# A second level of the seven-product scheme inside the first layer of a fused attention and snake MLP kernel

## The chip, the cores and the metric

The kernel runs on one core of one Trainium2 chip. The metric is the device time of one execution in microseconds: 910.94 us before the change, the median of three runs from 910.55 to 911.62 us. One profiled execution of the same kernel has a span of 908.3 us from its first to its last instruction. All data are float32.

## The reference, cut to what matters

Attention over pooled keys and values comes first (8 batches, 8 heads, 576 queries of width 64, 72 pooled keys), then a two-layer network with a snake activation on 4608 tokens.

```python
def _attn_ref(q, k, v):                       # q, k, v: (8, 8, 576, 64)
    k_p = k.reshape(B, H, Sp, 8, D).mean(axis=3)
    v_p = v.reshape(B, H, Sp, 8, D).mean(axis=3)
    scores = scale * np.matmul(q, k_p.transpose(0, 1, 3, 2))
    attn = softmax(scores)                    # written out in the source
    return np.matmul(attn, v_p)

def _moe_ref(x, w_in, w_out, alpha):          # x: (4608, 512), d_ff = 2048
    h = x @ w_in
    s = np.sin(alpha * h)
    g = h + s * s / (alpha + 1e-09)
    return g @ w_out
```

## The kernel before

The kernel works in nine units of 512 tokens. While unit u runs the first layer (`hidden`), the attention of batch u + 1 is interleaved with it. Both layers use the seven-product (Strassen-Winograd) scheme: eight block products become seven, paid for by additions. In the first layer the weights are cut into 2 x 2 blocks of 256 x 1024 and the tokens of a unit into 2 x 256. A unit has four groups J of 256 hidden rows, and a group has seven products, so a unit has 28 products in 28 slots (slot = 7 J + k). One product is four matmuls of a 128 x 128 weight block with 256 columns.

The sums that the scheme needs are formed in PSUM: ScalarE (ACT) copies the bank of product 1 to a second bank, TensorE (PE) accumulates product 6 onto the copy, ACT copies that to a third bank for product 7, and so on.

```python
for slot in range(7 * self.NJ):
    J, k = divmod(slot, 7)
    for f in self.left: f()              # what the slot before left to do
    for f in extra[slot]: f()            # the attention of the next batch
    ...
    def left0(): G.b6 = bank(); nc.scalar.copy(out=G.b6[:], in_=G.b1[:]); squares(Q)
    def left1(): self.finish(Q)                              # VectorE additions
    def left2(): self.store_g(Q); G.b7 = bank()
                 nc.scalar.copy(out=G.b7[:], in_=G.b6[:])    # b7 copy
                 nc.scalar.copy(out=G.p5[:], in_=G.b5[:])    # p5 copy
    def left3(): sin(G, 0, 0, G.b1); square(G, 0, 0)
    def left4(): add(G.g[:, 1, :, 1], G.b7[:], G.p5[:])
    def left5(): add(G.g[:, 0, :, 1], G.b6[:], G.p5[:]); sin(G, 1, 1, ...); add(G.g[:, 0, :, 0], ...)
    def left6(): sin(G, 0, 1, G.g[:, 0, :, 1]); ...; sin(G, 1, 0, G.b7)
    p = (1, 5, 6, 2, 7, 3, 4)[k]
    product(p, bank of p, k < 2)          # 4 matmuls, 128 x 128 by 256 columns
```

(The blocks `left0` to `left6` are shortened; Q is the group before G.) So the b7 copy of a group stands on ACT at the start of slot k = 3, and product 7 on PE in slot k = 4.

The attention enters through a table of slots. In units 1 to 6:

```python
at((3, 5)[i], A.two_scores, i)            # i = 0, 1
at((8, 9, 10, 10)[i], A.exp, i)           # i = 0 .. 3
at((9, 10, 11, 12)[i], A.norm, i)
at((12, 12, 13, 13)[i], A.turn, i)
at(14, A.move, range(4))                  # SBUF to SBUF transfers aM <- tr
at(25, A.all_values)                      # slot 25 is J = 3, k = 4
at(26, self.att[b + 1].k_t)
at(7, self.load_q, u + 3)
for part in range(4): at(22 + part, self.turn_q, u + 2, part)
```

`all_values` multiplies the attention weights with the pooled values (PE) and then puts the result, scaled, into the tokens of the next units (`to_x`, nine ACT instructions in units 1 to 6):

```python
def all_values():
    ...
    halves(ps[2], main[2][0], True); rest_of((0, 1))
    (nc.vector.tensor_copy if b > 1 else nc.scalar.copy)(out=<order>, in_=rest[:, 1, 0:1])
    for hp in (0, 3, 1): halves(ps[hp], main[hp][0], True)
    rest_of((2, 3))
    for hp in hps:                         # the four last matmuls, 32 x 512
        nc.tensor.matmul(ps[hp], w, x, start=False, stop=True)
    for hp in hps: to_x(ps[hp], hp, 0, 512)
    to_x(rest, slice(0, 4), 512, 64)

def to_x(...):
    nc.scalar.mul(out=x, in_=y, mul=1.0 / POOL)
```

Of the kernel before, what the change touches and what calls it, by code (L numbers as in the profile page):

```python
# [19 lines left out]
P = 128  # L20
# [20 lines left out]
class Kernel:  # L41
# [33 lines left out]
    def new_q(self, b):  # L75
        self.qm[b] = self.qp.tile([P, 5 * self.H * self.D], F32, name="q")
# [6 lines left out]
    def pairs_q(self, b, tiles):  # L83

        nc = self.nc
        if 0 in tiles:
            self.raw = self.q_views(self.qm[b])
            self.qm[b] = self.qp.tile([P, 5 * self.H * self.D], F32, name="q")
        x = self.qm[b][:].rearrange("p (t h e d) -> p t e h d", t=5, e=2, d=self.D)
        for t in tiles:  # L90
            n = P if t < 4 else 64
            raw = self.raw[0][:, :, t, :] if t < 4 else self.raw[1]
            nc.scalar.copy(out=x[:n, t], in_=raw.rearrange("p (e h) d -> p e h d", e=2))
# [108 lines left out]
    def turn_q(self, b, part):  # L202


        nc = self.nc
        qm = self.qm[b]
        main, rest = self.q_views(qm)
        if part == 0:
            self.tr = self.new_tr()
        tr = self.tr[:, 0:2560].rearrange("p (k x) -> p k x", k=2)  # L210
        if part == 0:
            for e in range(2):
                x = main[:, 4 * e:4 * e + 4].rearrange("p hp t (k i) -> p hp t k i", i=32).rearrange("p hp t k i -> p (hp t) k i")
                out = tr[:, :, 768 * e:768 * e + 512].rearrange("p k (n i) -> p n k i", i=32)
                nc.vector.transpose(out=out, in_=x)
            return
        if part == 1:
            nc.vector.transpose(out=tr[:64, :, 512:768].rearrange("p k (n i) -> p n k i", i=32),
                                in_=self.q_rows(qm).rearrange("p (n k i) -> p n k i", k=2, i=32))
            return  # L220
        self.qt[b] = qm[:]
        for a in ((0, 1), (2, 3))[part - 2]:
            for c in range(4):
                e, k = divmod(c, 2)
                w = 768 if a == e else 512
                to = 512 if a == e == 1 else self.q_at(a)
                at = 512 if a == e == 1 else 768 * e
                nc.sync.dma_start(out=qm[32 * c:32 * c + 32, to:to + w], in_=tr[32 * a:32 * a + 32, k, at:at + w])
# [14 lines left out]
    def attention(self, b):  # L243
# [22 lines left out]
        def q_t(i, copy=nc.scalar.copy):  # L266
# [3 lines left out]
            if b not in self.qt:  # L270
                self.qt[b] = self.qt_view(self.qp.tile([P, 5 * H * D], F32, name="q"))
# [105 lines left out]
        def q_head(hp):  # L377

            if hp == 0:
                self.qt[b] = self.qt_view(self.qp.tile([P, 5 * H * D], F32, name="q"))  # L380
# [73 lines left out]
        def a_head(g, banks):  # L454

            aM, aR = a0_views()
            for e in range(2):
# [4 lines left out]
                cp(out=aM[:, 2 * g + e, 0:4 * P], in_=ps.rearrange("k t n -> k (t n)"))  # L462
            ps = self.psum([P, 4, P], banks[2])
# [32 lines left out]
        def move(blocks, queue=nc.sync):  # L496

            tr = self.tr[:, 0:2944].rearrange("p (c s x) -> p c s x", c=2, s=2)
            for a in blocks:
                for s in range(2):  # L500
                    for c in range(2):
                        r, w = 64 * s + 32 * c, 704 if c else 736
                        queue.dma_start(out=self.aM[r:r + 32, a, 0:w], in_=tr[32 * a:32 * a + 32, c, s, 0:w])  # L503
# [78 lines left out]
        def all_values():  # L582
# [16 lines left out]
            (nc.vector.tensor_copy if b > 1 else nc.scalar.copy)(out=self.sm.tile([P, 1], F32, name="order")[:], in_=rest[:, 1, 0:1])  # L599
# [158 lines left out]

    def sums_of_x(self, u, n):
# [9 lines left out]
    def hidden(self, u, extra):  # L769

        nc = self.nc
        bank = lambda: self.bank([P, JW, TH])
        add = lambda o, x, y: nc.vector.tensor_tensor(out=o, in0=x, in1=y, op=OP.add)  # L773

        for slot in range(7 * self.NJ):
            J, k = divmod(slot, 7)
            for f in self.left:
                f()
            for f in extra[slot]:
                f()  # L780
            if k == 0:
                before = self.group
                G = self.group = SimpleNamespace(
                    u=u, J=J, b1=bank(), g=self.hp.tile([P, 2, JW, 2, TH], F32, name="h"),
                    s=self.hp.tile([P, 2, JW, 2, TH], F32, name="s", bufs=1))
            xT, bt = self.xT[u], self.bt[u]
            B = lambda i, j: xT[:, 2 * i:2 * i + 2, j * TH:(j + 1) * TH]

            def product(p, ps, start):
                x = {1: B(0, 0), 2: B(1, 0), 3: B(1, 1), 4: bt[:, 3], 5: bt[:, 0], 6: bt[:, 1], 7: bt[:, 2]}[p]  # L790
                for jj in range(JW):
                    f = J * JW + jj
                    for kk in range(2):
                        nc.tensor.matmul(ps[:, jj, :], self.A[p][:, kk, f * P:(f + 1) * P], x[:, kk, :],  # L794
                                         start=(start and jj == 0 and kk == 0), stop=(kk == 1), skip_group_check=True)

            def sin(G, i, j, src):
                for jj in range(JW):
                    f = i * self.K2 // 2 + G.J * JW + jj
                    nc.scalar.activation(out=G.s[:, i, jj, j, :], in_=src[:, jj], func=AF.Sin, scale=self.al[:, f:f + 1])  # L800

            def square(G, i, js):

                for jj in range(JW):
                    f = i * self.K2 // 2 + G.J * JW + jj
                    x = G.s[:, i, jj, js, :]
                    nc.scalar.activation(out=x, in_=x, func=AF.Square, scale=self.c[:, f:f + 1])  # L807

            early = lambda G: G.J == (0 if G.u else 1)

            def squares(G):
                if not early(G):
                    square(G, 0, 1)
                square(G, 1, slice(0, 2))

            self.squares = squares

            def left0(G=G, Q=before):
                G.b6 = bank()
                nc.scalar.copy(out=G.b6[:], in_=G.b1[:])  # L820
                if Q:
                    squares(Q)

            def left1(G=G, Q=before):
                if Q:
                    self.finish(Q)

            late = G.J == 0 and 0 < u < self.B - 1

            def left2(G=G, Q=before, late=late):  # L830
                if Q and not late:
                    self.store_g(Q)
                G.b7 = bank()
                nc.scalar.copy(out=G.b7[:], in_=G.b6[:])
                G.p5 = self.tp.tile([P, JW, TH], F32, name="p5")
                nc.scalar.copy(out=G.p5[:], in_=G.b5[:])

            def left3(G=G):
                sin(G, 0, 0, G.b1)
                square(G, 0, 0)  # L840

            def left4(G=G):
                add(G.g[:, 1, :, 1], G.b7[:], G.p5[:])

            def left5(G=G, Q=before, late=late):
                if late:
# [3 lines left out]
                add(G.g[:, 0, :, 0], G.b1[:], G.s[:, 0, :, 0])  # L850

            def left6(G=G):
                sin(G, 0, 1, G.g[:, 0, :, 1])
                if early(G):
                    square(G, 0, 1)
                sin(G, 1, 0, G.b7)

            self.left = [(left0, left1, left2, left3, left4, left5, left6)[k]]
            if k == 1:
                G.b5 = bank()  # L860
            p = (1, 5, 6, 2, 7, 3, 4)[k]
            product(p, getattr(G, {1: "b1", 5: "b5", 6: "b6", 2: "b1", 7: "b7", 3: "b6", 4: "b7"}[p]), k < 2)

    def finish(self, Q):
        add = lambda o, x, y: self.nc.vector.tensor_tensor(out=o, in0=x, in1=y, op=OP.add)  # L865
        add(Q.g[:, 1, :, 0], Q.b7[:], Q.s[:, 1, :, 0])
        add(Q.g[:, :, :, 1], Q.g[:, :, :, 1], Q.s[:, :, :, 1])
# [7 lines left out]
    def end_hidden(self):  # L875
        nc, Q = self.nc, self.group
        for f in self.left:
            f()
        self.squares(Q)
# [3 lines left out]
    def first_batch(self):  # L883
# [70 lines left out]
        A.a_head(0, (1, 7, 0))  # L954
        self.combine_w_in(0, (0,), nc.gpsimd)
        A.products_head(3)
        A.soft_exp(2)
# [15 lines left out]
    def carry(self, u):  # L973
# [6 lines left out]
        if u == 0:  # L980
# [36 lines left out]
            at(20, A.move, (3,), nc.scalar)  # L1017
            at(26, A.all_values)
            at(9, self.load_q, 2)
            at(14, self.load_q, 3)  # L1020
# [8 lines left out]
        if 0 < u < last:  # L1029
# [18 lines left out]
            if u + 3 <= last:  # L1048
                at(7, self.load_q, u + 3)
# [3 lines left out]
        if turn and u + 2 <= last:  # L1053
            for part in range(4):
                at(turn + part, self.turn_q, u + 2, part)
# [23 lines left out]
    def outputs(self):  # L1079
# [55 lines left out]
        def early(st):  # L1135
# [4 lines left out]
            if st["u"] == self.B - 1:  # L1140
                out(st["u"], 0, 1, t, 5, queues=(nc.sync, nc.scalar))
# [4 lines left out]
        def out(u, i, j, t, n0=0, n1=2 * T // 32, queues=(nc.sync, nc.sync)):  # L1146
# [7 lines left out]
            for a in range(4):  # L1154
                c = j * 2 * P + a * 64
                queues[a % 2].dma_start(out=self.out[r + 32 * n0:r + 32 * n1, c:c + 64].rearrange("(n k) c -> k n c", k=32),
                                        in_=o[32 * a:32 * a + 32, n0:n1].rearrange("k n h c -> k n (h c)"))

        def combine(st):
# [35 lines left out]
            else:  # L1195
# [4 lines left out]
                else:  # L1200
                    out(u, 0, 1, t, 0, 5, (nc.sync, nc.scalar))
# [69 lines left out]
    def run(self):  # L1271
        nc, tc = self.nc, self.tc
        pool = lambda s, n, b, **kw: s.enter_context(tc.tile_pool(name=n, bufs=b, **kw))
        with ExitStack() as top:
# [10 lines left out]
            with ExitStack() as one:  # L1285
# [8 lines left out]
                self.qp = pool(att, "qp", 2)  # L1294
# [12 lines left out]
                self.last = cb.tile([64, 640], F32, name="last")  # L1307
# [7 lines left out]
                self.bt, self.left, self.group, self.turn = {}, [], None, 2  # L1315
                self.R = {}
                self.first_batch()
                for u in range(self.NU):
# [63 lines left out]
```

## Time and profile before

| what | value |
|---|---|
| time, median of 3 | 910.94 us |
| span of the profiled execution | 908.3 us |
| ACT busy | 436.4 us (48%) |
| VectorE (DVE) busy | 665.6 us (73%) |
| GpSimd (POOL) busy | 170.8 us (19%) |
| data moved by DMA | 141.12 MB, mean 155 GB/s |

The first layer runs from about 20 us to 527 us of the span, the second layer follows. In the profile L794 is the matmul of the first layer's products, L1129 that of the second layer, L302 the scores, L592 and L605 the values, L519 the rescaling by `to_x`, L820 the copy of b1 to b6, L834 the copy of b6 to b7, L836 the p5 copy, L773 and L865 the additions of the first layer on DVE, L800 and L807 the sines and squares, L503 the issue of the transfers aM <- tr. A float32 matmul shows as two records, so a product is eight records. Matmuls overlap: the pace is the distance of one start from the next, not the duration of one record.

### The profile page before, as it was taken

How to read it: one execution, taken by the hardware profiler on the slowest of the kernel's cores; microseconds unless marked ns; L12 is line 12 of the kernel's file. 1: busy time of each engine (PE TensorE's matmuls, PEld its weight loads, DVE VectorE, ACT ScalarE, POOL GpSimd, SP SyncE). 2: the span in 40 equal slices, each digit the busy share in tenths (PEclk: the TensorE clock that was granted, in tenths of full speed). 3: DMA queues.
4: the chain of work that ended last, by engine and by line, in shares of the span. 5: the costliest groups of instructions: out<-in, count | busy, mean ns of one | idle time of the engine just before them, and what ended most of it. 6: DMA issues, size and time to landing. Idle time of an engine off the chain costs nothing.

```text
span 908.3 us, 17532 instructions
## 1 busy us (share of the span) xinstructions
PE 898.3 (99%) x6906; PEld 814.3 (90%) x6906; DVE 665.6 (73%) x1000; ACT 436.4 (48%) x998; POOL 170.8 (19%) x159
## 2 busy tenths in 40 slices
PE   8999999999999999999999999999999999999997
PEld 5787888888888888888888999999999999999997
DVE  7675766748567584663557899979798888889895
ACT  5695775867668676686876621111111111111111
POOL 4785350703408044130000000000000000000000
PEclk9999999999999999999999999999999999999999
DMA  9985766758667575548117247161618162534401
GB/s 263 242 249 153 210 170 193 194 174 233 175 176 189 165 204 170 146 116 313 73 74 249 94 127 220 37 213 40 222 27 226 37 190 72 171 92 128 134 15 40
DMA packets 128746, 141.12 MB, mean 155 GB/s; under 512 B 46920, under 2 KB 95704, under 8 KB 128664
## 3 DMA queue, kind: packets, MB, share of 16 engines
q1 hardware_dynamic: 126488, 138.03, 52.9%
q10 hardware_dynamic: 2176, 1.97, 0.8%
q8 instruction: 55, 0.90, 0.4%
q14 instruction: 27, 0.22, 0.1%
HBM read 75.37 MB, written 47.19 MB: 135 GB/s over the span
## 4 chain that ended last, share of the span: by engine, by line
PE 92%; DMA 2%; POOL 2%; SPq 1%; DVE 1%; ACT 1%; issue 0%; ACTq 0%; DVEq 0%; POOLq 0%
PE PS L794 44%; PE PS L1129 42%; PE PS L592 2%; PE PS L302 2%; DMA kvin<-in_v_dram 1%; SPq L659 1%; PE PS L605 1%; DMA a<-in_moe_w_in_dram 1%; POOL ex L359 1%; POOL kvin L127 0%; PE PS L904 0%; POOL as L665 0%; SPq L97 0%; ACTq L503 0%; PE PS L406 0%
## 5 line engine op out<-in xcount | busy, mean ns | idle before, releaser
L794 PE MATMUL PS<-home,a 128*128 128x256 f32 x1152 | 264.3, 381 | 1.2 <-ACT home L519 0.8
L794 PEld LDWEIGHTS PS<-home,a 128*128 128x128 f32 x1152 | 216.6, 190 | 37.4 <-issue 5.0
L794 PE MATMUL PS<-home,as 128*128 128x256 f32 x864 | 200.0, 380 | 0.7 <-ACT PS L820 0.7
L794 PEld LDWEIGHTS PS<-home,as 128*128 128x128 f32 x864 | 162.7, 190 | 23.7 <-issue 1.6
L1129 PE MATMUL PS<-s,wb 128*128 128x144 f32 x896 | 119.3, 286 | 0.4 <-ACT PS L1249 0.4
L1129 PEld LDWEIGHTS PS<-s,wb 128*128 128x128 f32 x896 | 113.7, 190 | 0.7 <-ACT PS L1249 0.6
L127 POOL TENSOR_TENSOR kvin<-kvin 96x768 f32<-96x768 f32 (+3 forms) x42 | 73.7, 1755 | 196.6 <-DMA kvin<-in_v_dram 195.0
L807 ACT ACTIVATE s<-s,c 128x256 f32<-128x256 f32 (+1 forms) x216 | 110.0, 572 | 0.0
L773 DVE TENSOR_TENSOR h<-PS,p 128x512 f32<-128x512 f32 x72 | 49.1, 684 | 78.3 <-PE PS L794 45.5
L800 ACT ACTIVATE s<-h,al 128x256 f32<-128x256 f32 x144 | 65.1, 503 | 55.5 <-DVE h L773 51.3
L1249 ACT COPY PS<-PS 128x144 f32<-128x144 f32 x56 | 14.7, 263 | 145.7 <-PE PS L1129 144.3
L800 ACT ACTIVATE s<-PS,al 128x256 f32<-128x256 f32 x144 | 60.1, 468 | 32.9 <-PE PS L794 18.4
L1129 PE MATMUL PS<-r,wb 128*128 128x144 f32 x512 | 73.2, 286 | 0.0
L1129 PE MATMUL PS<-s,a 128*128 128x144 f32 x512 | 73.2, 286 | 0.0
L865 DVE TENSOR_TENSOR h<-PS,s 128x512 f32<-128x512 f32 x36 | 24.6, 684 | 63.7 <-ACT s L807 63.7
L1129 PEld LDWEIGHTS PS<-r,wb 128*128 128x128 f32 x512 | 67.1, 190 | 0.1
L1129 PEld LDWEIGHTS PS<-s,a 128*128 128x128 f32 x512 | 67.0, 190 | 0.0
L1268 ACT COPY PS<-PS 128x144 f32<-128x144 f32 x56 | 14.7, 263 | 88.5 <-PE PS L1129 88.5
L1129 PE MATMUL PS<-s,we 128*128 128x144 f32 x384 | 54.9, 286 | 0.0
L1129 PE MATMUL PS<-x,wb 128*128 128x144 f32 x384 | 54.9, 286 | 0.0
L865 DVE TENSOR_TENSOR h<-h,s 128x1024 f32<-128x1024 f32 x36 | 50.6, 1405 | 0.0
L1129 PEld LDWEIGHTS PS<-s,we 128*128 128x128 f32 x384 | 50.3, 190 | 0.1
(188 smaller groups left out, 1187.0 us busy)
## 6 DMA issues: line engine op xcount, KB each, us to landing
g_bridge<-h SPq DMA_DIRECT2D x72, 512.0 KB
r<-g_bridge SPq DMA_DIRECT2D x31, 1152.0 KB
out_dram<-o SPq DMA_DIRECT2D x124, 72.0 KB
kvin<-in_k_dram SPq DMA_DIRECT2D x14, 576.0 KB
q<-in_q_dram SPq DMA_DIRECT2D x7, 1024.0 KB
kvin<-in_v_dram SPq DMA_DIRECT2D x14, 512.0 KB
aM<-tr SPq DMA_DIRECT2D x54, 92.0 KB
aM<-tr SPq DMA_DIRECT2D x54, 88.0 KB
```

Of the source, the lines that this page charges most:

```text
L127: self.nc.gpsimd.tensor_tensor(out=t[..., 0:w] if w > D else out, in0=t[..., 0:w], in1=t[..., w:2 * w], op=OP.add)
L302: nc.tensor.matmul(ps[e][r0 + r:r0 + r + q.shape[-1], h, :], q[s], kb[s, hp, :], start=True, stop=True)
L359: nc.gpsimd.tensor_tensor(out=E(i), in0=E(i), in1=sm.unsqueeze(2).to_broadcast([P, n, Sp]), op=OP.mult)
L592: nc.tensor.matmul(o[r:r + 64], w, x, start=start and i < 2, stop=False, skip_group_check=True)
L773: add = lambda o, x, y: nc.vector.tensor_tensor(out=o, in0=x, in1=y, op=OP.add)
L794: nc.tensor.matmul(ps[:, jj, :], self.A[p][:, kk, f * P:(f + 1) * P], x[:, kk, :], start=(start and jj == 0 and kk == 0), stop=(kk == 1), ...
L800: nc.scalar.activation(out=G.s[:, i, jj, j, :], in_=src[:, jj], func=AF.Sin, scale=self.al[:, f:f + 1])
L807: nc.scalar.activation(out=x, in_=x, func=AF.Square, scale=self.c[:, f:f + 1])
L865: add = lambda o, x, y: self.nc.vector.tensor_tensor(out=o, in0=x, in1=y, op=OP.add)
L1129: nc.tensor.matmul(out, W[:, J // 2, J % 2, :], A[:, J, :], start=(start and J == 0), stop=(J == self.NJ - 1), skip_group_check=True)
L1249: nc.scalar.copy(out=x1[:, 0, :], in_=x0[:, 1, :])
L1268: nc.scalar.copy(out=x1[:, 1, :], in_=x1[:, 0, :])
```

## The change

In units 1 to 6, three of the 28 products get a second level of the same scheme: product 5 of J = 2 and product 5 and product 1 of J = 3. Such a product, 2 x 2 blocks of 128, takes seven single matmuls of 128 columns in place of four matmuls of 256 columns (which are eight of 128). It is for saving PE one eighth of those products. The sums of weights are formed once by POOL (`inner_w_in`), those of the tokens by POOL at slot 2 of each unit (`inner_x`, eight subtractions of 128 x 128). The inner sums of products are formed by three ACT copies and one DVE addition for each product.

```diff
+    def inner_product(self, G, p, ps, y):
+        c = [ps[:, i, h * P:(h + 1) * P] for i in range(2) for h in range(2)]
+        f = ps.rearrange("p i (h t) -> p i h t", h=2)
+        def a():
+            products((1, 5), (y[:, 0], y[:, 1]), True)
+            nc.scalar.copy(out=f[:, 0], in_=y[:, 0:1].to_broadcast([P, 2, P]))   # 128x256
+            nc.scalar.copy(out=m5[p][:], in_=y[:, 1:2])                          # 128x128
+        def b():
+            products((6, 2), (c[1], c[0]))
+            nc.scalar.copy(out=c[2], in_=c[1])                                   # 128x128
+        def d():
+            products((7,), (c[2],))
+            nc.vector.tensor_tensor(out=f[:, :, 1], in0=x, in1=m5[p][:]..., op=OP.add)
+        def e():
+            products((3, 4), (c[1], c[2]))
```

The steps a, b, d, e are spread between halves of other products, and the order of copies, sines and squares is rewritten. What `left` did is now written out by slot. For J = 3 (`G.i1` is set; Q is J = 2):

```diff
+            if k == 0:   G.i5.b(); self.last_sines(Q, 0)
+            elif k == 2: product(G, 6, G.b6, part=(0, 1)); G.i5.d(); self.last_sines(Q, 1)
+                         square(Q, 1, 0); self.late = Q
+                         extras(); self.finish_before()
+                         product(G, 6, G.b6, part=(2, 3))
+            elif k == 3: square(Q, 1, 1); squares(Q, 0); extras()
+                         product(G, 2, G.b1); G.i5.e(); copy(G.p5[:], G.b5[:])
+            elif k == 4: extras()                            # slot 25: all_values
+                         copy(G.b7[:], G.b6[:])
+                         sin(G, 0, 0, G.b1)
+                         self.finish(Q, (1,)); self.store_g(Q)
+                         product(G, 7, G.b7, part=(0, 1))
+                         square(G, 0, 0)
+                         product(G, 7, G.b7, part=(2, 3))
```

For J = 2, product 4 of J = 1 is cut in halves, and the second half follows product 1 of J = 2:

```diff
+            if k == 0:   G.i5.a(); self.last_sines(Q, 0)     # sin(Q, 0, 1)
+                         product(G, 1, G.b1, True); product(Q, 4, Q.b7, part=(2, 3))
+            elif k == 1: copy(G.b6[:], G.b1[:]); self.last_sines(Q, 1); squares(Q, 0)
+            elif k == 2: product(G, 6, G.b6, part=(0, 1)); G.i5.b(); product(G, 6, G.b6, part=(2, 3))
```

(Both are shortened to the order of the calls.) The rest of the diff:

```diff
-        self.qm[b] = self.qp.tile([P, 5 * self.H * self.D], F32, name="q")   # pool of 2
+        self.qm[b] = self.q_tile(b > 1)                  # two named tiles, q0 and q1
...      # q0 then holds the inner sums of weights, q1 every later q
-            at(20, A.move, (3,), nc.scalar)
+            at(20, A.move, (3,), nc.scalar, (0,))        # unit 0: four requests on ACT,
+            at(21, A.move, (3,), nc.scalar, (1,))        # split over two slots
-            at(14, self.load_q, 3)                       # unit 0
+            at(23, self.inner_w_in)
-        A.a_head(0, (1, 7, 0))                           # prologue
+        A.a_head(0, (1, 7, 0), (0,))
...      # products_head(3) between the two parts
+        A.a_head(0, (1, 7, 0), (1,))
-                at(7, self.load_q, u + 3)
+                at(7, self.load_q, u + 2)
+            at(2, self.inner_x, u)
-                at(turn + part, self.turn_q, u + 2, part)        # 22, 23, 24, 25
+                at(((turn, turn + 1) if u == 0 else (23, 24))[part] if part < 2 else turn + part,
+                   self.turn_q, u + 2, part)             # units 1 on: 23, 24, 24, 25
+                if e == 0: self.finish_before()          # in turn_q, between its two halves
-            (nc.vector.tensor_copy if b > 1 else nc.scalar.copy)(out=<order>, ...)
+            nc.scalar.copy(out=<order>, ...)
-                    out(u, 0, 1, t, 0, 5, (nc.sync, nc.scalar))      # the last unit's output
+                    out(u, 0, 1, t, 0, 5, (nc.sync, nc.scalar, nc.scalar, nc.scalar))
```

`finish_before` is the addition of b7 and the squared sine of J = 2, which frees that bank for `all_values`.

## The prediction

> **What bounds the kernel now.** I read the page's busy shares, then the chain of waits in order of time, then the timeline of unit 2 around the values, then the groups by form for what a copy costs.
>
> ```profile
> PE 898.3 (99%) x6906; PEld 814.3 (90%) x6906; DVE 665.6 (73%) x1000; ACT 436.4 (48%) x998; POOL 170.8 (19%) x159
> PEclk9999999999999999999999999999999999999999
> PE 92%; DMA 2%; POOL 2%; SPq 1%; DVE 1%; ACT 1%; issue 0%; ACTq 0%; DVEq 0%; POOLq 0%
> ```
>
> PE is busy for 898.3 of 908.3 us at full clock, and the chain that ended last lies 92% on it. The 10 us that are left are in the first 20 us, around 74 us and after the last matmul. So anything that takes a matmul out of the middle pays in full, and anything that makes PE wait there costs in full: there is no slack to hide a wait in.
>
> ```profile
> 134.96 2.33 PE PS L592 x43
> 190.40 2.74 PE PS L592 x42
> 211.47 34.77 PE PS L794 x160
> 246.24 2.33 PE PS L592 x43
> 301.87 2.41 PE PS L592 x43
> 527.54 370.72 PE PS L1129 x3024
> ```
>
> The values (L592) begin 55.4 to 55.8 us apart: the period of a unit. Between them run 20 products of 8 records back to back: 34.77 us / 160 = 217.3 ns a record at 256 columns. The second layer gives 370.72 / 3024 = 122.6 ns at 144 columns. A period of 28 x 8 x 217.3 ns = 48.7 us for the products, 2.8 us scores, 3.4 us values and some tenths leaves nothing idle.
>
> ```profile
> 193.07 1.14 PE L605 MATMUL PS<-aM,vz 32*128 32x512 f32 x8
> 194.14 1.99 PE L794 MATMUL PS<-home,a 128*128 128x256 f32 x8
> 194.23 2.62 ACT L519 ACTIVATE home<-PS 128x320 f32<-128x320 f32 x9 [0.74 <-PE PS L605]
> 196.96 0.91 ACT L800 ACTIVATE s<-h,al 128x256 f32<-128x256 f32 x2
> ```
>
> These are start, duration, engine. The values end, PE goes at once (194.14) into product 7 of J = 3, and ACT begins its nine rescalings only then, at 194.23, and is held by them for 2.62 us. PE doesn't wait, because the copy that product 7 accumulates on was made two slots earlier.
>
> ```profile
> L820 ACT COPY PS<-PS 128x512 f32<-128x512 f32 x36 | 20.7, 575 | 19.3 <-PE PS L794 19.3
> L834 ACT COPY PS<-PS 128x512 f32<-128x512 f32 x36 | 20.6, 573 | 19.6 <-PE PS L794 19.4
> L1249 ACT COPY PS<-PS 128x144 f32<-128x144 f32 x56 | 14.7, 263 | 145.7 <-PE PS L1129 144.3 <-DVE h L773 1.4
> ```
>
> A copy of a whole bank takes 573 ns, one of 144 columns 263 ns, so about 0.84 ns a column: some 0.36 us for 256 columns and 0.25 us for 128.
>
> [...] (217.3 - 122.6) / 112 = 0.846 ns a column, which puts 128 columns at 122.6 - 16 x 0.846 = 109 ns. [...] here eight transposes with 128-column loads (15.33 us on) take 0.9 us, about 110 ns each, which agrees. [...] the longest wait of PE before is 1.1 us.
>
> **The change, part by part.**
>
> 1. *PE work removed.* An inner product is 7 matmuls, 14 records, at 110 ns: 1.54 us, in place of 8 x 217.3 = 1.74 us. Saved 0.20 us each, three in a unit, six units: 18 x 0.20 = 3.6 us. That is all that the change can win in the first layer. [...]
>
> 2. *A new wait at slot 25.* In J = 3 the b7 copy stands behind `extras()` in the program, and the extra of slot 25 is `all_values`. The built order on ACT is: p5 copy, order copy, the nine rescalings, b7 copy; on PE: the four last matmuls of the values, then at once product 7, which accumulates on b7 and waits for that copy. From the rows above: rescalings from 194.23 for 2.62 us, copy 0.57 us, and about 0.1 us from the end of a copy to the matmul that waits for it (at 74.00 us PE starts about 0.1 us after such a copy). That is 197.5 in place of 194.14: PE idle for 3.35 us. Nothing else of PE stands between, so all of it is lost. Units 1 to 6 have it, unit 0 (no second level) and units 7 and 8 (no attention) don't: 6 x 3.35 = 20.1 us.
>
> 3. *Waits at the head of J = 2.* PE does a (0.44 us), product 1 (1.74) and half of product 4 (0.87), then needs the b6 copy. On ACT the copy stands behind the two copies of a and the sines of J = 1, which wait for a DVE addition. In unit 3 before, that addition ended at 228.0 us against a start of J = 2 at 227.1, as DVE was still at the transposes of the weights. The last half of product 4 is moved, so J = 2 now starts 0.87 us earlier, at 226.2: PE asks for b6 at 226.2 + 3.05 = 229.3. The sines go from 228.06 for about 0.8 us, the copy from 228.87 to 229.44, PE from 229.6. Wait 0.3 us.
>
> 4. *The other waits of the inner products.* I walked the rest in the same way. Steps b, d and e each have 0.8 us or more of other products between them and the copy or addition they wait for, which take 0.25 to 0.7 us. Two places are tight: b6 of J = 3, copied after step e of product 1 and needed 0.9 us later, and the p5 copy before the fourth bank of the values, behind about 4 us of sines and squares. I give them 0.05 and 0.1 us. With part 3: 0.45 us a unit, 6 x 0.45 = 2.7 us.
>
> 5. *ACT, DVE, POOL as loads.* Per unit ACT gets 3 x (0.36 + 0.25 + 0.25) = 2.6 us more of 55 us in which it is about two thirds busy; DVE three additions of 256 columns; POOL eight subtractions of 128 x 128, about 0.45 us each by its 128 x 128 rows, some 9 us before they are needed. None is the bound.
>
> 6. *Unit 0 and the ends.* Four DMA requests hold ACT from 68.97 to 71.69 us, and the b6 copy and the copy before the last values come late for it: PE idles 0.70 us at 74.0 and 0.30 us at 76.3. Splitting the requests can return up to 1.0 us; with the other shifts of the prologue and the last outputs I take -0.7.
>
> 7. *q.* It is loaded one unit later into one buffer; from slot 7 to slot 23 there are about 29 us for 1 MB, when the core moves 150 to 250 GB/s. Its transposes start when the transfers aM <- tr have let the buffer go (242.66 in unit 3), as before. No cost.
>
> Sum: 910.9 - 3.6 + 20.1 + 2.7 - 0.7 = 929.4 us. Steps 2 and 4 can only grow from what I left out, so I say 930.
>
> **The rivals.**
>
> *The gain stays and the waits are hidden.* The time would be 910.9 - 3.6 - 0.7, near 907. For it: the steps are spread with care between halves of products, and `finish_before` is put between two transposes, which looks like tuning by a trace. Against it: the order on ACT puts b7 behind the rescalings, and these can't start before the values end, as the 0.74 us of waiting for L605 in the row shows.
>
> *ACT falls behind for good.* The page's ACT is busy eight tenths in some slices, with 96% in the 10 us of unit 2 that hold the exponentials. If three copies a product at the wrong moments make PE wait at each of b, d and e for 0.3 us, that is 9 waits or 2.7 us a unit, some 16 us on top: near 943. Against it: by J = 2 the timeline has ACT waiting for PE again (0.9 us before the b6 copy of J = 3).
>
> *The idle stretch slows the clock.* [...] I think it unlikely[...].
>
> *The loads bind at 128 columns.* If a record takes 125 ns and not 110, an inner product is no shorter than before: +3.6 us.
>
> **Range and chances.** Step 2 is sure to about 0.15 us a unit (1 us), step 4 goes from 0 to 7 us, step 6 from -1.5 to +1. That gives 925 to 936; the rivals, with a chance of about one in six together, widen it to 922 to 941. The border of 2% is 929.2 us, inside the range: slower by over 2% 0.56, within 2% 0.42, faster by over 2% 0.02, as the work removed is 0.4% of the time.
>
> **What would show it.** Right: in each of units 1 to 6 PE idles 3.3 to 3.4 us after the values, with the b7 copy as releaser, so PE's idle grows by some 20 us; the 128-column records stand about 110 ns apart; a few tenths at the first half of product 6 in J = 2 with the b6 copy as releaser; the clock stays at 1.00. Wrong: product 7 follows the values at once, or idle time of PE is spread over the inner steps, or it waits for q or aM transfers. A time below 915 would mean that step 2 fell.

## The result, and the profile after

The changed kernel takes 937.32 us (median of four, 936.28 to 939.05) against 911.07 us before: the ratio is 1.029, with a 95% interval of 1.0272 to 1.0308. The change makes the kernel slower by 26 us.

The first view is the page of the changed kernel: busy shares, granted clock and the chain that ended last. L832 is now the first layer's whole products, L1010 the matmuls of 128 columns, L1306 the second layer, L600 and L613 the values, L527 the rescalings, L808 the copies of a whole bank.

```profile
PE 906.9 (97%) x7014; PEld 823.6 (88%) x7014; DVE 675.0 (72%) x1012; ACT 450.6 (48%) x1070; POOL 209.5 (22%) x215
...
PEclk9999999999999899999999999999999999999999
...
PE 86%; DVE 5%; ACT 5%; DMA 2%; issue 1%; SPq 1%; DVEq 0%; ACTq 0%
```

PE has less to do, yet is busy for longer (906.9 against 898.3 us), idles for 30 us in place of 10, and its share of the chain falls from 92% to 86%. The granted clock is lower: one slice of PEclk shows an 8. The profiled execution is the slowest of the four (939.05 us, mean clock 0.988; the other three have 0.992), so it shows more of the low clock than they had. In order of time:

```profile
134.30 2.33 PE PS L600 x43
...
194.69 2.33 PE PS L600 x43
...
198.14 2.59 ACT home L527 x9
...
255.37 2.33 PE PS L600 x43
...
556.57 370.72 PE PS L1306 x3024
```

From unit 1 on the values now begin 60.4 and 60.7 us apart (59.3 to 61.7 in the units not shown), where they began 55.4 to 55.8 us apart; the second layer takes the same 370.72 us as before. The whole loss lies in units 1 to 6. A new link in the chain is ACT's nine rescalings, after the values. The timeline of unit 2 at that place (start, duration, what; in brackets the idle time before and its releaser):

```profile
196.97 1.14 PE L613 MATMUL PS<-aM,vz 32*128 32x512 f32 x8
198.12 2.61 ACT L527 ACTIVATE home<-PS 128x320 f32<-128x320 f32 x9 [2.09 <-PE PS L613]
200.52 0.70 ACT L808 COPY PS<-PS 128x512 f32<-128x512 f32 x1
...
201.27 3.21 PE L832 MATMUL PS<-home,a 128*128 128x256 f32 x8 [3.17 <-ACT PS L808]
```

Product 7 waits for the b7 copy, the copy stands behind the rescalings, and PE idles for 3.17 us. Then the eight records of product 7 take 3.21 us where they took 1.99 before. The windows after it tell why; the columns are the stretch, its length, PE's busy time, the granted clock, DMA share and GB/s:

```profile
201.00:203.00 2.00, 1.73 (x6) 0.72 0.49 122
203.00:205.00 2.00, 2.00 (x8) 0.50 0.38 95
205.00:207.00 2.00, 2.00 (x9) 0.92 0.42 104
207.00:209.00 2.00, 2.00 (x11) 1.00 0.93 345
```

After the idle stretch the granted clock is 0.50 from 201.90 to 205.31 us, for 3.41 us. The view of who waited for whom has one row that matters for PE:

```profile
PE PS L832 <- ACT PS L808: 22.2, 12, 3.2
```

Twelve waits, 22.2 us: six of 3.17 us at slot 25, and six of 0.43 to 0.77 us (3.2 us together) for the b6 copy at the start of J = 2. No row of PE names the small copies or the additions of the inner steps.

### The profile page after: what moved, and what is told of

It is laid out like the page before. It is cut to its first block, busy times and chain, and to the rows that moved or that the text cites. A ratio compares the mean times of both kernels' runs of the same rounds, so it can differ in the third digit from the quotient of the medians.

```text
span 937.3 us, 17929 instructions
## 1 busy us (share of the span) xinstructions
PE 906.9 (97%) x7014; PEld 823.6 (88%) x7014; DVE 675.0 (72%) x1012; ACT 450.6 (48%) x1070; POOL 209.5 (22%) x215
## 4 chain that ended last, share of the span: by engine, by line
PE 86%; DVE 5%; ACT 5%; DMA 2%; issue 1%; SPq 1%; DVEq 0%; ACTq 0%
PE PS L1306 40%; PE PS L832 36%; PE PS L1010 3%; PE PS L600 2%; ACT home L527 2%; DVE h L1032 2%; PE PS L308 2%; ACT PS L808 1%; DMA q<-in_q_dram 1%; DMA g_bridge<-h 1%; ACT s L987 1%; DVE sm L363 1%; PE PS L613 1%; DVE tr L491 1%; DVE h L807 0%
## 5 line engine op out<-in xcount | busy, mean ns | idle before, releaser
L832 PE MATMUL PS<-home,a 128*128 128x256 f32 x1104 | 264.1, 388 | 20.0 <-ACT PS L808 19.0
L832 PEld LDWEIGHTS PS<-home,a 128*128 128x128 f32 x1104 | 208.7, 193 | 55.2 <-ACT PS L808 25.1
L832 PE MATMUL PS<-home,as 128*128 128x256 f32 x768 | 185.9, 386 | 3.2 <-ACT PS L808 3.2
L832 PEld LDWEIGHTS PS<-home,as 128*128 128x128 f32 x768 | 144.0, 193 | 25.0 <-ACT PS L808 5.6
L1306 PE MATMUL PS<-s,wb 128*128 128x144 f32 x896 | 119.3, 286 | 0.4 <-ACT PS L1426 0.4
L1306 PEld LDWEIGHTS PS<-s,wb 128*128 128x128 f32 x896 | 113.7, 190 | 0.7 <-ACT PS L1426 0.6
L987 ACT ACTIVATE s<-s,c 128x256 f32<-128x256 f32 (+1 forms) x228 | 113.5, 563 | 0.0
L131 POOL TENSOR_TENSOR kvin<-kvin 96x768 f32<-96x768 f32 (+3 forms) x42 | 71.5, 1703 | 69.2 <-DMA kvin<-in_v_dram 67.6
L1306 PE MATMUL PS<-r,wb 128*128 128x144 f32 x512 | 73.2, 286 | 0.0
L1306 PE MATMUL PS<-s,a 128*128 128x144 f32 x512 | 73.2, 286 | 0.0
L1306 PEld LDWEIGHTS PS<-r,wb 128*128 128x128 f32 x512 | 67.1, 190 | 0.1
L1306 PEld LDWEIGHTS PS<-s,a 128*128 128x128 f32 x512 | 67.0, 190 | 0.0
L808 ACT COPY PS<-PS 128x512 f32<-128x512 f32 x72 | 42.1, 584 | 35.0 <-PE PS L832 30.4
L1306 PE MATMUL PS<-s,we 128*128 128x144 f32 x384 | 54.9, 286 | 0.0
L1306 PE MATMUL PS<-x,wb 128*128 128x144 f32 x384 | 54.9, 286 | 0.0
L1306 PEld LDWEIGHTS PS<-s,we 128*128 128x128 f32 x384 | 50.3, 190 | 0.1
```

Source lines behind the costliest of these rows:

```text
L131: self.nc.gpsimd.tensor_tensor(out=t[..., 0:w] if w > D else out, in0=t[..., 0:w], in1=t[..., w:2 * w], op=OP.add)
L808: copy = lambda o, x: nc.scalar.copy(out=o, in_=x)
L987: self.nc.scalar.activation(out=x, in_=x, func=AF.Square, scale=self.c[:, f:f + 1])
L1306: nc.tensor.matmul(out, W[:, J // 2, J % 2, :], A[:, J, :], start=(start and J == 0), stop=(J == self.NJ - 1), skip_group_check=True)
```

## The experiments

The theory after the result: the b7 copy behind the rescalings costs 19 us of idle PE, the halved clock after each of those stretches costs most of the rest, and the inner products gain about what they should but lose it again in the b6 wait. The rivals: the inner steps or ACT's extra load make the loss; another part of the change (the single q buffer, POOL's sums) makes some; the clock has no part in it. Each ratio below is against the kernel before on the same chip, which takes 910.67 us beside e1 to e4 and 909.97 us beside e5 to e7. Views and counts by unit are of one profiled execution of each kernel.

### e1: the b7 copy ahead of the rescalings

```diff
-                extras()
                 if G.i1:
                     copy(G.b7[:], G.b6[:])
+                extras()
+                if G.i1:
                     sin(G, 0, 0, G.b1)
```

> The changed kernel with one line moved: the b7 copy of J = 3 stands ahead of the extras of slot 25, so ahead of the rescalings. If the wait behind the rescalings (6 x 3.17 us of idle PE in the trace) and the slower clock after it make the loss, PE goes from the values into product 7 at once, the clock is 1.00 throughout and the time is 911.1 - 3.6 (inner products) + 3.2 (6 x 0.53 us wait for b6 in J = 2) - 1.2 (unit 0) = 909.5 us, from 908 to 912. If instead the inner products' own waits or ACT's extra load make it, the time stays above 925.

Measured: 911.13 us, ratio 1.0008 (0.9999 to 1.0017), clock 0.999. All of the loss hangs on this one line. PE's row of 22.2 us becomes this:

```profile
PE PS L832 <- ACT PS L808: 3.7, 6, 1.2
```

The six waits at slot 25 are gone, those for b6 are left. The time is 0.5 us above the kernel before on that chip, where 1.6 us below was expected, so the gain of the inner products does not show yet.

### e2: the wait alone, in the kernel before

```diff
-                nc.scalar.copy(out=G.b7[:], in_=G.b6[:])
+                if not behind(G):                # J = 3 of units 1 to 6
+                    nc.scalar.copy(out=G.b7[:], in_=G.b6[:])
...
+            if k == 4 and behind(G):             # after the extras, before product 7
+                nc.scalar.copy(out=G.b7[:], in_=G.b6[:])
```

> The kernel before with one line moved: in units 1 to 6 the b7 copy of J = 3 stands behind the rescalings. No inner products, nothing else of the change. If that wait and the clock after it are the whole loss, it costs 6 x 3.2 = 19 us of idle PE and some 7 us by the clock: 936 to 939 us. If the clock falls for another reason (the inner products' gaps), there is no fall here and the time is 930. If the inner products make most of the loss, it stays under 925.

Measured: 939.28 us, ratio 1.0313 (1.0298 to 1.0328), clock 0.989. The waits of PE and two of the six stretches after them (units 2 and 3; columns as above):

```profile
PE PS L794 <- ACT PS L864: 19.0, 6, 3.2
```

```profile
203.00:209.00 6.00, 5.90 (x21) 0.72 0.42 103
263.40:269.00 5.60, 5.54 (x27) 1.00 0.47 116
```

Without one inner product the same 19.0 us of idle time and the same fall of the clock come about, in five of six units; unit 3 is the one that was spared. So the inner products have no part in the fall, and the misplaced copy costs 28.6 us by itself, more than the whole change.

### e3: matmuls to fill the idle stretch, a miss

```diff
                     self.store_g(Q)
+                    free = self.PS[:, (self.turn + 1) % 5, 256:512]
+                    for _ in range(24):
+                        nc.tensor.matmul(free, self.full[:], <full, 256 columns>, start=True, stop=True)
                 product(G, 7, G.b7, part=(0, 1))
```

> The changed kernel with 24 bf16 matmuls of ones, 256 columns each, put on PE into an unused half bank just ahead of product 7 of J = 3, so that PE works through some 2.6 of the 3.2 us in which it waits. Their results are used by nothing. If the idle stretch slows the clock, the clock stays at 1.00 and the time falls by about 7 us to 930, with the wait for the copy as it was. If the clock has no part in the time, it stays at 937; if the extra matmuls delay product 7, it is above.

Measured: 947.96 us, ratio 1.0406 (1.039 to 1.0421), clock 0.992 to 0.998. It did not test what it was made for. In unit 2:

```profile
201.47 4.21 PE L936 MATMUL PS<-full 128*128 128x256 bf16 x24 [2.67 <-ACT home L527]
```

The half bank that they write shares its bank with the last rescaling, and they wait for it: the stretch is only cut to 2.67 us, and then the fill stands in front of product 7. One thing can be read all the same: in five units the fill took 2.78 us (product 7 starts 2.61 or 2.62 us after its first matmul, so 109 ns a matmul of 256 columns), here 4.21, so after 2.67 us of idle time the clock fell in one unit of six. This execution is the fastest of the five (944.18 us, clock 0.998); the others have 0.992 to 0.996, so more time at the low clock.

### e4: all of the change but the inner products

```diff
-            if two and J > 1:                    # G.i5
+            if False:
-            if two and J == 3:                   # G.i1
+            if False:
```

and the same for the next group and for the halves of product 4, so that J = 2 and J = 3 run as J = 1 does.

> The changed kernel without the inner products: products 1 and 5 of J = 2 and J = 3 are whole again and their copies and sines stand as in the other groups, all else of the change (single q buffer, POOL sums, split requests in unit 0, output queues) stays. If the rest of the change is worth only the end of the waits in unit 0, the time is 911.1 - 1.2 = 910 us, from 909 to 911.5. If the later q load or the POOL sums cost something, it is above 912 with waits for q or with longer DVE additions.

Measured: 909.92 us, ratio 0.9991 (0.9982 to 1.0). Taken together, the q buffer, POOL's sums, the place of the order copy, the outputs and the split requests in unit 0 cost nothing: the time is 0.8 us lower, with an interval from 1.6 us lower to none. What each of them is worth was not tried. In the changed kernel's unit 0 the two waits of 0.70 and 0.30 us are gone:

```profile
73.29 1.99 PE L832 MATMUL PS<-home,as 128*128 128x256 f32 x8
75.21 0.64 PE L583 MATMUL PS<-last_t,vm 64*64 64x64 f32 x16
```

PE goes from the transposes at 73.14 into the product at 73.29, and from that into the last values of batch 0 at 75.21, with no bracket on either line. The trace of e4 has lost them too, but there a wait for a DVE addition at 55.44 us is 1.07 us long, 0.26 before, so not all of unit 0's gain need arrive.

### e5: the fill in b7's own bank

```diff
                 extras()
                 if G.i1:
+                    for _ in range(20):
+                        nc.tensor.matmul(G.b7[:, 0, :], self.full[:], <full, 256 columns>, start=True, stop=True)
                     copy(G.b7[:], G.b6[:])
```

The extra matmuls write b7 before the copy overwrites it, but the output is not the reference's; why was not shown. The order and the sizes of all other instructions are those of the change.

> The changed kernel with 20 bf16 matmuls of ones (256 columns each, about 2.1 us at full clock) that write b7's own bank right after the values, before the copy overwrites it; they wait for nothing, and the copy order is as in the change. PE's idle stretch falls from 3.2 to about 1 us while product 7 still begins when the copy is done. If the idle stretch halves the clock, the clock stays at 1.00 and the time falls by about 7 us to 930. If the clock has no part, the time stays at 937.

Measured: 930.89 us, ratio 1.0228 (1.0214 to 1.0242), clock 0.998 to 1.0. Unit 2:

```profile
197.86 2.36 PE L931 MATMUL PS<-full 128*128 128x256 bf16 x20
197.95 2.61 ACT L527 ACTIVATE home<-PS 128x320 f32<-128x320 f32 x9 [2.09 <-PE PS L613]
200.34 0.71 ACT L808 COPY PS<-PS 128x512 f32<-128x512 f32 x1
...
201.10 1.99 PE L832 MATMUL PS<-home,a 128*128 128x256 f32 x8 [0.88 <-ACT PS L808]
```

From the end of the values (197.86) to product 7 (201.10) it is 3.2 us as in the change, but the extra matmuls take 2.36 us of it and PE idles only for the last 0.88 us, product 7 takes 1.99 us again, and the time is 6.4 us lower than the change's as it stands, 5.3 us if each is taken against the kernel before on its own chip (20.9 us above it here, 26.2 us in the change). That is the price of the clock; product 7 still waits for the copy.

### e6: the b7 copy between the rescalings

```diff
             for n, hp in enumerate(hps):
                 to_x(...)
+                if n == 1 and self.hook: self.hook()     # the b7 copy, after four of nine
```

> The changed kernel with the b7 copy between the fourth and the fifth of the nine rescalings: PE idles for about 1.9 us in place of 3.2. The wait alone gives 911.1 + 6 x 1.9 = 922.5 us. If a stretch of 1.9 us still lets the clock fall in some units, the clock is under 0.999 and the time lies between 924 and 930; if the fall needs about 3 us, the clock stays at 0.999 and the time is 922 to 923.

Measured: 923.95 us, ratio 1.0152 (1.0138 to 1.0166), clock 0.995 to 0.998. Product 7 in unit 2 and in unit 5, and the clock after the latter:

```profile
197.75 1.99 PE L834 MATMUL PS<-home,a 128*128 128x256 f32 x8 [1.77 <-ACT PS L810]
...
370.77 3.65 PE L834 MATMUL PS<-home,a 128*128 128x256 f32 x8 [1.77 <-ACT PS L810]
```

```profile
371.00:375.00 4.00, 4.00 (x14) 0.58 0.45 109
375.00:379.00 4.00, 4.00 (x20) 1.00 0.49 137
```

The stretch is 1.77 us in all six units, and the clock falls in one of them. The time lies between the two bands that were expected, just under that for a fall in some units (924 to 930); the clock below 0.999 says that there were some. It goes with the length of the wait: 1.4 us less waiting in each unit is 8.4 us, and buys 12 us (14.0 us above the kernel before, the change 26.2).

### e7: the b6 copy first as well

```diff
             if k == 0:
-                    self.last_sines(Q, 0 if G.i5 else 2)       # ahead of product 1
+                    if not G.i5: self.last_sines(Q, 2)
             elif k == 1:
                 copy(G.b6[:], G.b1[:])
-                self.last_sines(Q, 1); squares(Q, 0)           # J = 2
+                self.last_sines(Q, 2)
             elif k == 2:
                 product(G, 6, G.b6, part=(0, 1)); G.i5.b()
+                squares(Q, 0)
```

on top of e1 (shortened to the order of the calls).

> The version of e1_b7_first in which, at the start of J = 2, the b6 copy also goes ahead of the sines of J = 1, and the squares of J = 1 behind the small copy of step b. If the b6 wait in J = 2 (3.7 us in six units in the trace of e1_b7_first) is what ate the inner products' gain, it goes and the time is 911.1 - 3.5 = 907.6 us, from 906.5 to 908.5, faster than the kernel before by 0.3%. If the wait only moves to a later step (the small copies or the p5 copy), the time stays at 910 to 911.5. If a 128-column record is no faster than half of a 256-column one, PE's busy time does not fall and the time stays above 910.

Measured: 906.91 us (median of six, 905.7 to 909.77), ratio 0.9965 (0.9953 to 0.9977): 3.1 us faster than the kernel before, and the fastest of all versions by the ratio. The start of J = 2 in unit 2 of e1, where the copy stands behind the sines:

```profile
172.87 0.36 ACT L1015 COPY PS<-PS 128x256 f32<-128x256 f32 x1 [0.57 <-DVE h L807]
...
173.30 0.92 ACT L981 ACTIVATE s<-h,al 128x256 f32<-128x256 f32 x2
174.11 0.59 ACT L808 COPY PS<-PS 128x512 f32<-128x512 f32 x1
...
174.75 1.13 PE L832 MATMUL PS<-home,as 128*128 128x256 f32 x4 [0.43 <-ACT PS L808]
```

and of e7, where it stands ahead of them:

```profile
172.84 0.57 ACT L808 COPY PS<-PS 128x512 f32<-128x512 f32 x1
173.33 0.91 ACT L981 ACTIVATE s<-h,al 128x256 f32<-128x256 f32 x2
...
173.51 1.09 PE L832 MATMUL PS<-home,as 128*128 128x256 f32 x4
```

The bracket on PE's line is gone, and no other PE wait of the inner steps has come in its place. In the same trace a later unit shows the inner matmuls at full pace:

```profile
345.39 0.38 PE L1011 MATMUL PS<-home,a 128*128 128x128 f32 x2
345.61 0.39 PE L1011 MATMUL PS<-ex,q 128*128 128x128 f32 x2
345.83 1.03 PE L832 MATMUL PS<-home,as 128*128 128x256 f32 x4
```

Two records every 0.22 us: 110 ns at 128 columns. The values of units 5 and 6 of e7 begin 55.20 and 55.23 us after those of the unit before, in e4 55.55 and 55.56; those of unit 3 55.06 us, in e4 55.55.

## Why the prediction was right, and where it was off

The direction and the range held: 937.3 us lies between 922 and 941, and slower by over 2% was the likeliest of the three outcomes. The point, 930, is 7 us too low, and the steps by themselves gave 925 to 936, which 937.3 lies above: it is inside the range only because the rivals had widened it. One of the signs named for being right failed too, that the clock stays at 1.00. By its steps:

| step | predicted, us | measured, us | from |
|---|---|---|---|
| 1, PE work removed | -3.6 | -3.6 by the pace of 110 ns | trace of e7 |
| 2, wait at slot 25 | +20.1 | +19.0 | six waits of 3.17, the change; 19.0 also in e2 |
| 3, b6 wait in J = 2 | +1.8 | +3.2 | 22.2 - 19.0, the change |
| 4, other waits | +0.9 | no PE row; 0.1 to 0.3 a unit in gaps, about 1.3 by estimate | periods of e7 and e4 |
| 6, unit 0 and the ends | -0.7 | -0.8 (-1.6 to 0) | e4 |
| 7, q | 0 | 0 | e4 |
| rival, halved clock | in the range only | +5.3 to +6.4 | change less e5 |

These sum to 24.4 to 25.5 us, against the 26.2 measured; no more can be asked of it, as the rows come from different runs and the start of the values of unit 0 alone lies anywhere from 79.9 to 81.6 us in these traces.

*Step 2* was right in mechanism and nearly in size, and e1 and e2 show it from both sides: taken out, the loss is gone; put alone into the kernel before, it is all there. The 0.18 us that I had too much come from the rescalings and the copy overlapping: the copy starts at 200.52, 0.2 us before the 2.61 us of the rescalings are over. It takes 0.70 us, not 0.57, which gives back part of that.

*The term that was mis-sized is the clock.* I named it as a rival, sized it by an estimate of mine that no run had shown, called it unlikely, which no run had shown either, and kept it out of the sum. It came in five of six units of the profiled run and cost 5.3 to 6.4 us, about 1 us a unit. In six units of each profiled run, the clock fell in none after 0.88 us (e5), in one after 1.77 (e6), in one after 2.67 (e3), in five after 3.17 (the change, and five again in e2). So a shorter stretch was not safe, only less often hit.

What went with the fall is where the stretch lay. By the clock record of its trace, the granted clock of the changed kernel falls in the first layer from 1.00 to 0.50 at 140.46, 201.90, 263.33, 321.36 and 444.24 us, which are 18, 18, 17 and 36 times 3.413 us apart, and it stays low for 3.41 us, in unit 4 for 6.83. So a grid with a step of 3.413 us can be laid over the trace through these points. Three steps of unit 1 of the change, with the fall at 140.46, then the two that share the stretch of unit 5, after which it did not fall (columns as above):

```profile
137.05:140.46 3.41, 0.66 (x8) 1.00 0.49 119
140.46:143.87 3.41, 2.99 (x7) 0.50 0.49 121
143.87:147.28 3.41, 3.41 (x19) 1.00 0.56 161
379.39:382.80 3.41, 1.69 (x30) 1.00 0.48 118
382.80:386.21 3.41, 1.96 (x10) 1.00 0.51 121
```

The step before the fall has 2.75 us without work, those of unit 5 1.72 and 1.45. In e6, where all six stretches are 1.77 us long, with the grid laid through its own fall at 370.94, the first step is of unit 4, without a fall, the other two of unit 5, with it:

```profile
309.50:312.92 3.42, 1.95 (x32) 1.00 0.40 95
367.53:370.94 3.41, 1.64 (x25) 1.00 0.48 120
370.94:374.36 3.42, 3.42 (x9) 0.50 0.46 111
```

The stretch of unit 5 lies whole in one step; in the other units the larger part in one step is 1.47 us at most. In the first layer of the change, e2, e3 and e6, the twelve steps after which the clock fell had 1.77 to 3.17 us of idle time; the steps at full clock after which it did not fall had 1.73 us at most, but for one of 1.86 (unit 3 of e2; the ends of matmuls in the trace are modelled). So a stretch of 1.77 us, about half of a step, was enough in the one unit where it lay whole in one.

*Step 3* was too small: 0.43 to 0.77 us, not 0.3. I had the two copies of step a run while the sines waited for the DVE addition. In the trace of e1 the first of them itself waits 0.57 us for that addition, since it writes the bank the addition reads; so copies, sines and b6 copy all stand behind it. e7 moves the b6 copy ahead of the sines, and its wait is no longer a row of PE.

*Step 1* was right in size: an inner product takes 14 x 110 ns. What the walk of step 4 didn't see is gaps of about 0.1 us and less at some of the hand-overs, too short to show as idle time, since records overlap (in the rows of e7, two records take 0.38 us from 345.39, and the next start at 345.61). Against the 0.60 us a unit removed, the period of e7 is shorter than that of e4 by 0.49 us in unit 3 and by 0.33 to 0.35 us in units 5 and 6. In the latter two some 0.2 us lie at the b6 hand-over of J = 2: in unit 5 the first record of product 6 starts 0.31 us after the one before it (at 338.99), where the pace is 0.22, and its first four take 0.97 us, not 0.87. What the other gaps come from was not tried.

*The rivals.* ACT's load and the inner steps: fell by e1 and by the missing PE rows. Loads that bind at 128 columns: fell by the 110 ns. q and POOL: fell by e4. The rival by which all waits are hidden, 4.3 us under the kernel before, is reached most of the way by e7, 3.1 us under it, but only after two copies were moved.

## What to carry to other kernels

Where PE is the bound, what counts is the place in the other engine's queue of the one copy that PE waits for next: a copy that is ready two slots earlier should not stand behind a batch of work that can't start before PE is done with its own (here 2.61 us of rescalings, for which PE idled 3.17 us in each of six units). Count an idle stretch with the slow clock after it, here 3.2 us and about 1 us more, and compare a saving with the waits that its own bookkeeping makes: 3.6 us of matmuls paid for three copies a product, and the kernel with them, 0.8 us of other gains included, was faster by 0.35% only once both copies stood ahead of the sines and the rescalings.

## What the runs showed of the hardware that was not expected

- The granted clock fell from 1.00 to 0.50 after idle stretches of PE as short as 1.77 us, in one unit of six (e6); at 3.17 us it fell in ten of twelve (the change and e2). In the first layer of the change, all its falls and rises stand at multiples of 3.413 us from one another. The twelve falls in the first layer of four traces (the change, e2, e3, e6) came where PE had idled for 1.77 us or more of the 3.413 us before; once, in e2, 1.86 us went without a fall.
- With 2.36 us of such a stretch filled with matmuls that nobody needs, the clock stayed at 0.998 to 1.0 and the kernel took 5.3 to 6.4 us less, though product 7 started no earlier (e5, whose output is not the reference's).
- Matmuls that write one half of a PSUM bank waited, in this program, for ACT's read of the other half (e3: 2.67 us of idle time ended by the last rescaling). The wait is one that the program asks for; no run shows whether the chip needs it.
